# High parts of one expert weight and of four far-key tiles: from GpSimd to ScalarE

## The chip, the cores and the metric

One core of one Trainium2 chip. The metric is the device time of one execution in microseconds (us); several runs are taken and their median is shown. TensorE (PE), VectorE (DVE), ScalarE (ACT), GpSimd (POOL) and SyncE (SP, which issues the DMAs) each work through a queue of their own, in order.

## What is computed

Three stages, one after the other, on 2304 tokens of 512 features:

```python
scores = q @ k.T / sqrt(64)            # 4 batches, 8 heads, 576 positions, head size 64
scores = where(block_i >= block_j, scores, -1e9)   # causal by blocks of 64
x = softmax(scores) @ v                # -> x[2304, 512]
p = probs / probs.sum(-1)
y = sum_e p[:, e] * (relu(x @ w1[e]) @ w2[e])      # 4 experts, w1 512x1024, w2 1024x512
h = y @ w_in                           # 512 -> 1024
s = h * softmax(h)
out = layernorm(s) * g_ln @ w_out      # 1024 -> 512
```

## The kernel before, in words

Every operand of a matrix product is **split** into a high part (the value rounded to a narrower type) and a low part (what the rounding left), and a product takes three matmuls: high by high, high by low, low by high. So each weight, key, query, value and probability tile costs an instruction that makes the high part and one that makes the low part. Which engine makes which is written out by hand:

- **Weights**: `w_steps` (line 177) loads a weight into a staging tile of 128x4096, squares its four quarters on ScalarE to find a scale, and its inner `split` then makes, quarter by quarter (128x1024), the high part (GpSimd at L231 if `hi_eng is gp`, else ScalarE at L235) and the low part on VectorE (L238). On the ScalarE path `bg_` and `paced_a` may tie the instruction behind a marked ScalarE instruction in the schedule. The first expert's first weight is `next_w(gp)` at line 1241, its second one `next_w(gp, place_raw="w2")` at line 1242. All later weights already take ScalarE for the high part.
- **Keys and queries**: `parts` (line 788) makes high (L796 on ScalarE, L798 on GpSimd) and low (L800) by a two-letter `mode`: the first letter names the engine of the high part ("a" ScalarE, "p" GpSimd), the second that of the low part ("d" VectorE, "p" GpSimd). With `cut` it does so in two halves.
- **Far keys**: the first batch's keys come in two pieces. The near 192 columns are needed first (`k_near`), the far 384 (`k_far`, line 824, eight heads) from token tile 3 on. `k_far` uses mode "pp", so both parts are GpSimd's, 128x384 high and 64x384 low.

```python
if mode[0] == "a":
    act.activation(out=hi, in_=raw, func=AF.Copy)
else:
    gp.tensor_scalar(out=hi, in0=raw, scalar1=1.0, scalar2=1.0, op0=ALU.mult, op1=ALU.mult)
eng = vec if mode[1] == "d" else gp
eng.tensor_tensor(out=lo[ps], in0=raw[ps], in1=hi[ps], op=ALU.subtract)
```

**Order of the work.** `plan` (which the change touches) lists, for each step of attention, which loads and splits come with it; far keys of heads 0 and 1 come with step 6, 2 and 3 with step 7, and so on to step 9. A hand-written string of tokens sets the order of the first steps; after it a loop emits one attention step at a time, three background tasks (weight squares and splits) with each, and expert work between them by a running balance of costs. The order in which each engine finally gets its instructions is set by the scheduler of the framework, which runs a timing model of its own and follows dependencies and priorities; only SyncE's order is pinned in the first part. Raw key, raw value and similar loads share three buffers (`kr`), so a load waits in SyncE's queue until a GpSimd or ScalarE reader has released one.

One attention step is: scores on PE (`sps`, L920, L923), row maximum on VectorE (L935), its scaling (`nm`, L939), exponential on ScalarE (L979), probability split (`hl`: ScalarE L992, VectorE L993), a transposing DMA (`pT`), and the product with the values on PE (`pv`, L1021). The expert products are `hps` (L375) and `ops` (L397); the latter needs the second weight's four quarters.

Of the kernel before, what the change touches and what calls it, by code (L numbers as in the profile page):

```python
# [63 lines left out]
def tile_kernel(  # L64
# [38 lines left out]
    vec, act, gp, sync = nc.vector, nc.scalar, nc.gpsimd, InOrder(nc.sync)  # L103
# [8 lines left out]
    ap = ctx.enter_context(tc.tile_pool(name="acc", bufs=1))  # L112
# [609 lines left out]
    def next_w(hi_eng=None, eng=None, place_raw="stage"):  # L722
        i = nw[0]
        nw[0] += 1
        inv = iw[:, i:i + 1]
        tag, eng = f"w{i % 3}", eng or sync
        if i == 2 * len(LOADS):
            return w_steps("w_in", wf["w_in"], 15, inv, tag, eng)
        if i == 2 * len(LOADS) + 1:
            return w_steps("w_out", wf["w_out"], 15, inv, tag, eng, rows=gl)  # L730
        j, second = divmod(i, 2)
        j = LOADS[j]
        e = ORDER[j]
        key = ("w2" if second else "w1", e)
        if j >= E:
            inv = iw[:, 2 * e + second:2 * e + second + 1]
        pre, post = w_steps(
            key, (w2 if second else w1)[e], 15 if second else 10, inv, tag, eng, hi_eng=hi_eng, place_raw=place_raw,
            known=j >= E, less=j > E and not second,
        )  # L740
        return pre, [lambda: wcol.__setitem__(key, inv)] + post


    class Attention:
# [339 lines left out]
        def at(self, n, loads, *uses):  # L1084
            self.todo.append((n, loads, uses))

        def plan(self):
            first, at = self.first, self.at
            L = lambda f, *a: lambda: f(*a)
            for t in range(3, NTILE):  # L1090
                for c in range(2):
                    at(first[t] - 2 + 2 * c, ("qr", L(self.q_load, t, c)), L(self.q_prep, t, c))
            n = first[2]
            for h in range(NH):
                at(n + h // 2 + 2, ("kr", L(self.k_far_load, h)), L(self.k_far, h))
            for j in range(2, 5):
                at(first[j + 1] - 1, (None, None), L(self.v_split, 0, j))
            for b in range(1, NB):
                n = first[2 + 4 * b]
                f4 = n - 8  # L1100
                for j in range(5):
                    at(f4 - 5 + j, ("kr", L(self.v_load, b, j)), L(self.v_square, b, j))
                at(f4, (None, None), L(self.v_scale, b, 5))
                for j, m in enumerate([n - 2, n + LAG, n + LAG, n + LAG + 2, n + LAG + 3]):
                    at(m, ("kr", L(self.v_load, b, j)), L(self.v_split, b, j))
                for h in range(NH):
                    at(f4 + 1 + h, ("kr", L(self.k_load, b, h)), L(self.k_prep, b, h))
# [131 lines left out]
        xps[1].tile([128, 3, 512], F32, tag="xT1", name="vr"), xps[1].tile([128, 2, 512], F32, tag="xT3", name="vr"),  # L1239
    ]  # L1240
    p0, q0 = next_w(gp)
    p1, q1 = next_w(gp, place_raw="w2")

    def load_near(odd):
        at1.raws["near"] = near
        c = 0 if odd else S - NEAR
        src = kT[:, 0].rearrange("d (p x) s -> d p x s", x=2)[:, :, odd, c:c + NEAR]
        sync.dma_start(out=near.rearrange("d (p x) s -> d p x s", x=2)[:, :, odd], in_=src)

    def load_v(v, a, b):  # L1250
        sync.dma_start(out=v, in_=vC[0, :, a:b])
        for j in range(a, b):
            at1.raws["v", 0, j] = [v[:, j - a]]
# [5 lines left out]
    def norm():  # L1259
# [9 lines left out]
        n=[lambda: load_near(0), lambda: load_near(1)], v=[lambda: load_v(vrs[0], 0, 3), lambda: load_v(vrs[1], 3, 5)], p=[load_p],  # L1269
# [62 lines left out]
    p1, q1 = todo["x"], todo["X"]  # L1332
# [28 lines left out]
    for j in range(1, 5):  # L1361
        us = phase_units(j, GROUPS[j // E], psh)
        n = len(us)
# [46 lines left out]
    n = len(moe)  # L1410
# [209 lines left out]
```

## Time and profile before

| | |
|---|---|
| median of 3 runs | 1089.95 us (1089.48 to 1091.84) |
| the profiled execution | 1090.29 us |
| its span in the trace | 1088.5 us |
| PE busy | 1041.5 us, 96% of the span |
| VectorE busy | 776.3 us, 71% |
| ScalarE busy | 511.1 us, 47% |
| GpSimd busy | 208.1 us, 19%, 280 instructions |

How to read the rows below. In the page's picture of 40 slices a slice is 27.2 us and a digit the busy share in tenths. In the table by stretches the columns are: the stretch, its length, busy time (and instructions) of PE, PE's weight loads, VectorE, ScalarE and GpSimd, then the granted PE clock, the mean busy share of the DMA engines and GB/s. A line of a timeline is: start, duration, engine, source line, operation, tile written <- tiles read, and in brackets how long the engine had stood idle and what released it. A line of the chain is start, length and who held it. A line of a group of instructions is: source line, engine, operation, shapes, count, then busy time, mean ns of one, idle time before them.

### The profile page before, as it was taken

The numbers are of one execution on the slowest core, as the hardware profiler recorded it, in microseconds if no ns is written. First come the engines' busy times: TensorE is split into PE (matmuls) and PEld (weight loads), VectorE is DVE, ScalarE is ACT, GpSimd is POOL, SyncE is SP. The second block draws the span as 40 slices with busy tenths as digits, with TensorE's granted clock in tenths as the row PEclk, the third lists the DMA queues.
The fourth block names the chain that finished last, engine by engine and source line by source line (L and its number), as shares of the span: only waits on it lengthen the run. The fifth ranks groups of instructions, "written<-read, shape, count | busy, mean of one in ns | idle before, by whom it ended". The sixth has DMA issues, their size and how long they took to land.

```text
span 1088.5 us, 20680 instructions
## 1 busy us (share of the span) xinstructions
PE 1041.5 (96%) x8088; PEld 657.0 (60%) x8088; DVE 776.3 (71%) x1758; ACT 511.1 (47%) x1108; POOL 208.1 (19%) x280
## 2 busy tenths in 40 slices
PE   4679899999999999999899999999999999999998
PEld 4556666656655655655476777776766674444444
DVE  6879677748767765545786557665879558999883
ACT  5757578546755454532353334231446353323322
POOL 4967733534237311000000000000000000000000
PEclk9989999999999999999999999999999999999999
DMA  9978997566677865235331211330346312435233
GB/s 295 277 175 167 241 201 189 143 173 172 158 178 174 186 112 129 56 90 157 122 97 51 77 47 55 117 136 30 98 145 167 77 24 36 88 88 106 60 87 87
DMA packets 225745, 137.96 MB, mean 127 GB/s; under 512 B 184560, under 2 KB 193008, under 8 KB 225648
## 3 DMA queue, kind: packets, MB, share of 16 engines
q1 hardware_dynamic: 225648, 136.65, 50.3%
q8 instruction: 63, 1.03, 0.4%
q14 instruction: 34, 0.28, 0.1%
HBM read 79.47 MB, written 12.06 MB: 84 GB/s over the span
## 4 chain that ended last, share of the span: by engine, by line
PE 84%; DMA 6%; DVE 4%; POOL 3%; ACT 1%; issue 1%; SPq 0%; DVEq 0%; ACTq 0%; POOLq 0%
PE ops L397 31%; PE hps L629 14%; PE hps L375 14%; PE o L1536 9%; PE h L1470 9%; PE pv L1021 3%; DMA pT<-hl 3%; PE sps L920 2%; PE sps L923 2%; DMA xT<-xh 1%; POOL ks L800 1%; DMA raw<-in_w_dram 1%; DMA x2T<-xh 1%; DMA near<-in_kT_dram 1%; DMA vraw<-in_vC_dram 1%
## 5 line engine op out<-in xcount | busy, mean ns | idle before, releaser
L397 PE MATMUL ops<-wt,hch 128*128 128x512 f16 x1728 | 393.1, 379 | 2.4 <-DVE wt L238 1.4
L397 PEld LDWEIGHTS <-hch 128*128 128x128 f16 x1728 | 166.1, 98 | 187.4 <-issue 6.7
L375 PE MATMUL hps<-xT,wt 128*128 128x384 f16 (+1 forms) x1536 | 216.1, 290 | 6.3 <-DVE hch L386 3.9
L375 PEld LDWEIGHTS <-wt 128*128 128x128 f16 x1536 | 126.5, 100 | 64.4 <-issue 6.1
L979 ACT ACTIVATE p<-sps,nm 128x320 f32<-128x320 f32 (+3 forms) x120 | 70.1, 587 | 85.1 <-DVE nm L939 75.4
L993 DVE TENSOR_TENSOR hl<-p,hl 128x320 f16<-128x320 f32 (+3 forms) x120 | 75.6, 650 | 37.3 <-ACT hl L992 37.2
L629 PEld LDWEIGHTS <-S 128*128 128x128 f16 x1152 | 96.0, 98 | 3.0 <-issue 0.9
L1536 PE MATMUL o<-wt,lt 128*128 128x512 f16 (+1 forms) x456 | 95.6, 368 | 0.0
L1470 PE MATMUL h<-wt,x2T 128*128 128x512 f16 x432 | 95.5, 379 | 0.0
L238 DVE SCALAR_TENSOR_TENSOR wt<-stage,ws,wt 128x1024 f16<-128x1024 f32 (+1 forms) x64 | 82.9, 1304 | 7.4 <-ACT wt L235 4.3
L422 DVE SCALAR_TENSOR_TENSOR acc<-ops,coef,acc 128x512 f32<-128x512 f32 x54 | 40.4, 748 | 66.4 <-PE ops L397 66.3
L920 PE MATMUL sps<-ks,qhi 128*128 128x288 f32 (+3 forms) x160 | 69.1, 433 | 10.7 <-DVE hl L993 7.5
L629 PE MATMUL hps<-T,S 128*128 128x192 f16 x864 | 76.3, 246 | 0.0
L629 PEld LDWEIGHTS <-wt 128*128 128x128 f16 x864 | 72.8, 98 | 5.8
L642 ACT ACTIVATE stu<-hps 128x384 f32<-128x384 f32 x72 | 34.6, 482 | 86.5 <-PE hps L629 86.3
L1536 PEld LDWEIGHTS <-lt 128*128 128x128 f16 x456 | 44.6, 98 | 48.9
L1470 PEld LDWEIGHTS <-x2T 128*128 128x128 f16 x432 | 42.3, 98 | 51.0
L386 DVE SCALAR_TENSOR_TENSOR hch<-hps,hch 128x384 f16<-128x384 f32 (+1 forms) x98 | 52.8, 540 | 21.9 <-ACT hch L385 21.8
L647 ACT ACTIVATE hch<-stc 128x384 f16<-128x384 f32 x72 | 37.4, 521 | 63.5 <-DVE stc L655 63.2
L385 ACT ACTIVATE hch<-hps 128x384 f16<-128x384 f32 (+1 forms) x98 | 46.9, 481 | 39.5 <-PE hps L375 39.4
L1021 PE MATMUL pv<-v,pT 128*128 128x64 f16 x1392 | 56.6, 196 | 8.9 <-DMA pT<-hl 8.8
L1021 PEld LDWEIGHTS <-pT 128*128 128x128 f16 x1392 | 51.6, 100 | 20.5 <-DMA pT<-hl 10.8
(163 smaller groups left out, 1534.6 us busy)
## 6 DMA issues: line engine op xcount, KB each, us to landing
stage<-in_w_dram SPq DMA_DIRECT2D x50, 512.0 KB, 5.9
raw<-in_qT_dram SPq DMA_DIRECT2D x34, 256.0 KB, 3.1
vraw<-in_vC_dram SPq DMA_DIRECT2D x30, 256.0 KB, 3.2
raw<-in_kT_dram SPq DMA_DIRECT2D x24, 288.0 KB, 3.5
raw<-in_w_dram SPq DMA_DIRECT2D x24, 256.0 KB, 4.1
raw<-in_w_in_dram SPq DMA_DIRECT2D x8, 512.0 KB, 4.7
raw<-in_w_out_dram SPq DMA_DIRECT2D x8, 512.0 KB, 4.2
stage<-wf SPq DMA_DIRECT2D x8, 512.0 KB, 6.6
```

The lines of the kernel that those rows point to most:

```text
L238: stage["last"] = vec.scalar_tensor_tensor(out=lo, in0=r, scalar=stage[key, "s"], in1=hi, op0=ALU.mult, op1=ALU.subtract)
L375: pe.matmul(ps[:, j * n:j * n + n], w[:, a, kk, f * 128:(f + 1) * 128], x[:, b * KD + kk, c0:c0 + n], start=(m == 0), stop=(m == 3 * KD - 1),)
L385: marks["A"] = nc.scalar.activation(out=h[:, 0, :n], in_=ps[:, :n], func=AF.Relu)
L386: marks["D"] = nc.vector.scalar_tensor_tensor(out=h[:, 1, :n], in0=ps[:, :n], scalar=0.0, in1=h[:, 0, :n], op0=ALU.max, op1=ALU.subtract)
L397: pe.matmul(ps, hch[f][:, a, o0:o0 + 128], w[:, b, f, :], start=(m == 0), stop=(m == 3 * KF - 1))
L629: i = pe.matmul(ps[x][:, jj * HT:jj * HT + HT], lhs(a, kk, jj), rhs(b, kk), start=start, stop=(m == 5), skip_group_check=not first or jj > 0,)
L920: pe.matmul(o, q, rhs, start=True, stop=False)
L979: act.activation(out=src if direct else dst, in_=src, func=AF.Exp, bias=nm[:, j + x:j + x + 1], scale=SCALE, accum_out=sums[:, h:h + 1],)
L993: anc["D"] = vec.tensor_tensor(out=lo, in0=pf, in1=hi, op=ALU.subtract)
L1021: pe.matmul(o, tt[:, a * nch + c, :], v[:, bb, hs], start=(m == 0), stop=(m == total - 1))
L1470: pe.matmul(ps[:, half], x[:, a * KD + kk, c:c + 128], w[:, b, kk, half * 512:half * 512 + 512], start=(m == 0), stop=(m == 3 * KD - 1),)
L1536: pe.matmul(ps, tt[:, x * KF + f], w[:, y, f, c], start=(m == 0), stop=(m == 3 * KF - 1))
```

## The change

The far keys of the odd heads (four of eight) get mode "ap": ScalarE makes the high part, GpSimd still the low part. The first expert's second weight loses `gp`, so ScalarE makes its four high quarters. Nothing else is edited; the halves that `parts` cuts for later keys and queries are the same in both kernels.

```diff
             for h in range(NH):
-                at(n + h // 2 + 2, ("kr", L(self.k_far_load, h)), L(self.k_far, h))
+                at(n + h // 2 + 2, ("kr", L(self.k_far_load, h)), L(self.k_far, h, "ap" if h % 2 else "pp"))
...
     p0, q0 = next_w(gp)
-    p1, q1 = next_w(gp, place_raw="w2")
+    p1, q1 = next_w(place_raw="w2")
```

## Rows read from the trace of the kernel before

**Rows 1.** The page's picture of the span in 40 slices.

```profile
PE   4679899999999999999899999999999999999998
...
POOL 4967733534237311000000000000000000000000
```

**Rows 2.** The table by stretches.

```profile
50.00:57.00 7.00, 5.14 (x76) 4.56 (x74) 6.85 (x18) 5.18 (x14) 6.92 (x7) 1.00 0.59 185
57.00:66.40 9.40, 7.21 (x61) 4.09 (x59) 6.62 (x12) 2.80 (x10) 9.11 (x9) 1.00 0.50 120
66.40:76.40 10.00, 7.21 (x78) 6.14 (x76) 7.50 (x17) 7.46 (x22) 7.09 (x9) 0.73 1.03 211
...
82.00:136.00 54.00, 47.95 (x645) 36.76 (x644) 43.28 (x92) 35.43 (x87) 41.69 (x58) 1.00 0.94 202
136.00:1088.50 952.50, 942.46 (x6984) 576.77 (x6981) 670.15 (x1516) 422.98 (x869) 109.70 (x158) 1.00 0.45 112
```

**Rows 3.** The chain that ended last: first and last of 25 pieces on GpSimd, and the next.

```profile
33.72 2.08 POOL wt L231
...
60.54 2.10 POOL ks L800
62.66 2.78 DMA vraw<-in_vC_dram
```

**Rows 4.** Groups of GpSimd's instructions, 50 to 72 us.

```profile
L231 POOL TENSOR_SCALAR wt<-stage,ws 128x1024 f16<-128x1024 f32 x4 | 4.9, 1221 | 0.2
...
L798 POOL TENSOR_SCALAR ks<-raw 128x384 fp32r<-128x384 f32 x5 | 3.7, 745 | 0.0
```

**Rows 5.** GpSimd's timeline, two low parts of far keys.

```profile
60.54 2.09 POOL L800 TENSOR_TENSOR ks<-raw,ks 64x384 fp32r<-64x384 f32 x1
...
70.01 0.99 POOL L800 TENSOR_TENSOR ks<-raw,ks 64x384 fp32r<-64x384 f32 x1
```

**Rows 6.** VectorE's timeline around the second weight's low parts.

```profile
50.20 0.15 DVE L143 RECIPROCAL ws<-iw 128x1 f32<-128x1 f32 x1
...
60.49 1.28 DVE L238 SCALAR_TENSOR_TENSOR wt<-stage,ws,wt 128x1024 f16<-128x1024 f32 x1 [1.48 <-POOL wt L231]
61.70 0.15 DVE L939 TENSOR_SCALAR nm<-sps 128x2 f32<-128x2 f32 x1
...
63.89 1.52 DVE L238 SCALAR_TENSOR_TENSOR wt<-stage,ws,wt 128x1024 f16<-128x1024 f32 x1 [1.30 <-POOL wt L231]
```

**Rows 7.** PE's timeline, its waits for the second weight and the far keys.

```profile
61.83 1.24 PE L397 MATMUL ops<-wt,hch 128*128 128x512 f16 x5 [0.94 <-DVE wt L238]
...
68.11 0.41 PE L920 MATMUL sps<-ks,qhi 128*128 128x320 f32 x1 [0.46 <-POOL ks L800]
...
71.05 0.64 PE L920 MATMUL sps<-ks,qhi 128*128 128x320 f32 x1 [1.61 <-POOL ks L800]
```

**Rows 8.** The table by stretches, finer, where the granted clock falls.

```profile
68.00:72.00 4.00, 1.97 (x17) 1.34 (x17) 3.58 (x10) 3.45 (x10) 3.06 (x5) 0.88 1.15 150
72.00:76.00 4.00, 3.59 (x41) 3.45 (x42) 2.38 (x5) 2.13 (x7) 2.51 (x4) 0.50 1.11 323
76.00:80.00 4.00, 4.00 (x55) 3.35 (x54) 2.47 (x8) 2.75 (x10) 0.00 (x0) 0.77 1.11 215
```

**Rows 9.** ScalarE: group and single instructions that price the added work.

```profile
L235 ACT ACTIVATE wt<-stage,ws 128x1024 f16<-128x1024 f32 x4 | 4.6, 1148 | 0.0
...
L992 ACT ACTIVATE hl<-p 128x320 f16<-128x320 f32 x8 | 3.4, 460 | 0.0
```

**Rows 10.** ScalarE's timeline, two single instructions.

```profile
5.13 0.63 ACT L796 ACTIVATE qhi<-qv 128x512 fp32r<-128x512 f32 x1 [3.12 <-DMA qv<-in_qT_dram]
...
61.88 0.53 ACT L979 ACTIVATE p<-sps,nm 128x320 f32<-128x320 f32 x1 [4.78 <-DVE nm L939]
```

**Rows 11.** SyncE's last load of a far key, and such loads' time to landing.

```profile
60.04 0.53 SPq L94 DMA_DIRECT2D raw<-in_kT_dram  x1
...
raw<-in_kT_dram SPq DMA_DIRECT2D x8, 192.0 KB, 3.4
```

## The prediction

> **What bounds the kernel now.** I read the picture of the span first. PE is busy in nine tenths of nearly every slice, but not in the first three, and there GpSimd reaches its peak, nine tenths in the second slice [rows 1]. So PE sets the pace of the rest, and time can be won only where PE stands idle early on. The table by stretches says how much: from 57.0 to 66.4 us PE is idle for 9.40 - 7.21 = 2.19 us, from 66.4 to 76.4 for 10.00 - 7.21 = 2.79, together 4.98. From 82 to 136 it is idle for 6.05 us, and in all the 952.5 us that follow for 10.0 [rows 2].
>
> Next the chain that ended last. From 33.72 to 62.64 us it stays on GpSimd for 25 pieces, and goes on by a raw-value load [rows 3]. GpSimd's queue is thus the bound of that stretch: in 50 to 66.4 it is busy for 6.92 + 9.11 of 16.4 us, while ScalarE works 5.18 + 2.80 [rows 2]. The timelines show how the queue reaches PE. VectorE stands 1.48 and 1.30 us for a high quarter of the second weight, and the scaling of a row maximum (L939) is queued behind such a low quarter; ScalarE's exponential waits for that scaling with 4.78 us of idleness before it [rows 6, 10]. PE itself waits 0.94 us for the weight and 0.46 and 1.61 us for far keys [rows 7].
>
> The price of these waits does not end with the waits: the granted clock falls to 0.50 of full speed, the lower of the two levels (1.2 GHz), in 72 to 76, after PE was busy only 1.97 us of the 4 before [rows 8].
>
> **The change part by part.** The sum is made against the profiled execution's own 1090.29 us; the median of the runs is 0.34 lower, so the last step takes 0.34 off.
>
> *Removed from GpSimd.* Four high quarters of the weight, 4.9 us by their group. Four far-key high parts, by the mean of the five in the same stretch 4 x 0.745 = 3.0 us [rows 4]. Its queue gets 7.9 us shorter before the last far key, whose low part now begins at 70.01 and ends at 71.0 [rows 5].
>
> *Added to ScalarE.* Four quarters at 1.148 us, the price of the same instruction for later weights: 4.6 us. Four high parts of 128x384: no row has this size with this output; below stands 0.460 for 320 columns, above 0.63 for 512 columns of the same output type. I take 0.52, nearer to the first in size, so 2.1 us; ends 1.8 and 2.5 [rows 9, 10]. The 6.7 us lie beside other work: ScalarE has 7.00 - 5.18 + 9.40 - 2.80 = 8.4 us free from 50 to 66.4 [rows 2], 4.78 of them in one piece before the exponential [rows 10]. If that cover is gone, the exponentials pay (third rival).
>
> *The first term: VectorE no longer waits for GpSimd.* The scale `ws` is there at 50.35 [rows 6]. Even if all of ScalarE's 5.18 us of 50 to 57 go first [rows 2], the third quarter is ready by 50.35 + 5.18 + 3 x 1.148 = 59.0 and the fourth by 60.1; VectorE now begins the third low quarter at 60.49 and the fourth at 63.89. The two waits of 1.48 and 1.30 go, and the second scaling behind them, its exponential, its transpose and the `pv` that waits for this move up by 2.78 us. Nothing on VectorE is added: it makes the same low parts. What is late next is VectorE itself, busy 6.85 of 7.00 us in 50 to 57 [rows 2]. So -2.8; ends 0 (the exponentials lose on ScalarE what VectorE wins) and -2.8.
>
> One row speaks of a further gain: a far-key low part on GpSimd took 2.09 us where the last took 0.99, and it began 0.05 us after VectorE began a low quarter of 1.28 [rows 5, 6]. So these two delay each other, and fewer instructions on GpSimd may mean shorter ones on VectorE. I count nothing for it in the sum; one quarter took 1.52 and another 1.28 [rows 6], so if all four of VectorE's low quarters lost that difference it would be 4 x 0.24 = 1.0 us, which I keep for the lower end. The Trainium skill, "SBUF — State Buffer", section "SBUF: two separate sides", holds that GpSimd and VectorE instructions with two SBUF inputs exclude each other for a whole instruction, while ScalarE never waits; the trace agrees in that one pair (2.09 against 0.99), and by the rule the first term would be nearer to -3.8 than to -2.8.
>
> *The second term: far keys.* PE's waits of 0.46 and 1.61 us [rows 7] go, since GpSimd's queue ends 7.9 us earlier, or as early as the last load allows: it is issued at 60.04, once a GpSimd low part has released the buffer, and lands 3.4 us later [rows 11]. SyncE's queue moves up with the buffers, as does the raw-value load behind them at 62.66 [rows 3]. But the `pv` and scores behind these waits hang on the exponentials as well, and those move up only by the first term. So I count 0 beyond it; ends 0 and -2.2 (4.98 us of idleness less 2.8).
>
> *The third term: the clock.* At the full level the 3.59 us in 72 to 76 would be 1.8 shorter, the 4.00 in 76 to 80 by 0.23 x 4.0 = 0.9, and the 1.97 before by 0.12 x 1.97 = 0.2 [rows 8]. That is 2.9 us, if PE no longer stands idle for 2.03 of 4 us ahead of them. The first term takes away more than half of the 4.98 us of idleness, so I take half: -1.5; ends 0 and -2.9.
>
> *The edits' other ends.* The first odd far key's high part leaves GpSimd before 43 us too, ahead of the value splits; a part's time, 0.745 us, is the most that it can win, and I count it at nothing, for the bound only. No DMA is added or removed.
>
> Sum: -2.8 - 1.5 = -4.3, so 1086.0 on the profiled execution's scale and **1085.7** on the median's. At the far end -2.8 - 1.0 - 2.2 - 2.9 - 0.7 = -9.6.
>
> **The rivals.** What a measurement of this kernel can tell from no change is about 0.2%, 2.2 us.
>
> *The transposes give it back.* DMA is busy for 1.03 of its time from 66.4 to 76.4 and 0.94 from 82 to 136 [rows 2]. If those transfers end when they do now, PE comes earlier and waits there: the idle 6.05 us of 82 to 136 would grow by what was won. Against this: the DMA engines are at 0.59 and 0.50 in 50 to 66.4 [rows 2], because their issues wait for GpSimd's buffers; they can start earlier too. By this rival some 1 us is left: 1089.0.
>
> *ScalarE in GpSimd's place.* ScalarE's queue is in order. If the four weight quarters (4.6), two far keys (1.0) and a wait for the last far-key load (it lands at 60.04 + 3.4 = 63.4, 1.5 us after the exponential at 61.88) stand in one block ahead of that exponential, this is 7.1 us against 4.78 of idleness [rows 9 to 11]. It decides from the point where the exponential starts later than 61.88, and costs 7.1 - 4.78 = 2.3 us, passed to PE through `pv`: 1092.3, slower. Against it: the far keys of the later heads are emitted steps later, and a scheduler by readiness would put the exponential ahead of a far key that has not landed.
>
> *The change doesn't do what it says* is nearly excluded: without `gp`, `split` has the ScalarE path that every later weight uses, and four such instructions are in the trace [rows 9]. The scheduler may however order other things anew; that can win or lose part of the 10.0 us of idleness behind 136 us [rows 2], and is why the chances aren't higher.
>
> **How the numbers follow.** My forecast, GpSimd's chain shortened and most of it kept: 0.60. The transposes, or something like them, give it back to within 0.2%: 0.22. ScalarE in GpSimd's place, or a worse order: 0.18. The time is that of the likeliest, 1085.7. The range goes from 1081.5, which leaves out only the case that nearly every far end comes true (1080.4), up to 1092.3, the third rival's time; the forecast's own range is 1081.5 to 1087.8. Faster by over 0.2% 0.60, within 0.2% 0.22, slower by over 0.2% 0.18.
>
> **What would show it.** After the change GpSimd should have eight instructions fewer and some 8 us less work, and the chain should leave it before 55 us. VectorE's waits for GpSimd at L238 should be gone; PE's idleness in 57 to 76 should fall from 4.98 to about 2, and the stretch at half clock be shorter. The products with the second weight should end some 3 us earlier. I am wrong if the exponential at 61.88 starts no earlier, if ScalarE shows a weight quarter or a far key with idleness ahead of it just before an exponential, or if PE's waits for `pT` behind 82 us grow by what the front wins.

## The result, and the profile after

The changed kernel is **slower** by 0.8%: 1099.27 us median (1094.09 to 1103.96, 5 runs) against 1090.06 (1089.48 to 1091.98, 5 runs), ratio of the means 1.0077 with 95% interval [1.0047, 1.0106]. The forecast was 1085.7 with a range up to 1092.3. The profiled execution took 1100.92 us, its span is 1099.1 us, 10.6 more than before.

The page of the changed kernel, busy times:

```profile
PE 1046.4 (95%) x8088; PEld 660.6 (60%) x8088; DVE 775.0 (71%) x1758; ACT 516.7 (47%) x1116; POOL 196.9 (18%) x272
```

GpSimd lost its 8 instructions and 208.1 - 196.9 = 11.2 us. PE has the same 8088 matmuls as before and is busy 1046.4 - 1041.5 = 4.9 us longer, at a lower clock (0.989 granted on the mean over the span, 0.997 before). The other 10.6 - 4.9 = 5.7 us are idleness. The table by stretches says where (stretch, length, busy time of PE, PE's weight loads, VectorE, ScalarE, GpSimd, granted clock, DMA share, GB/s):

```profile
50.00:57.00 7.00, 3.71 (x44) 3.16 (x41) 6.43 (x12) 7.00 (x15) 5.53 (x6) 0.79 0.64 189
57.00:66.40 9.40, 9.40 (x75) 5.44 (x74) 6.39 (x13) 7.35 (x20) 4.22 (x7) 0.80 0.78 199
66.40:76.40 10.00, 10.00 (x131) 7.50 (x128) 7.64 (x22) 8.72 (x26) 2.81 (x5) 1.00 0.72 180
76.40:82.00 5.60, 3.63 (x36) 2.21 (x33) 4.99 (x14) 4.12 (x6) 0.00 (x0) 1.00 1.21 159
82.00:136.00 54.00, 46.43 (x595) 38.00 (x596) 37.58 (x80) 31.73 (x79) 34.80 (x52) 0.91 0.89 188
136.00:200.00 64.00, 56.51 (x597) 39.55 (x595) 45.02 (x100) 45.77 (x116) 27.18 (x37) 0.95 0.87 191
200.00:1099.10 899.10, 890.68 (x6417) 540.51 (x6414) 627.64 (x1421) 378.89 (x762) 88.54 (x126) 1.00 0.42 106
```

and the stretch of the kernel before that [rows 2] holds only as part of a longer one:

```profile
136.00:200.00 64.00, 61.99 (x634) 41.04 (x631) 46.64 (x105) 47.93 (x117) 21.42 (x33) 1.00 0.83 195
```

From 57.0 to 76.4 us PE's idleness fell from 4.98 us [rows 2] to 0: more than was forecast. But it grew on either side: from 7.00 - 5.14 = 1.86 to 3.29 us in 50 to 57, and from 0 to 1.97 in 76.4 to 82. Two waits make this (PE's timeline, changed kernel):

```profile
55.14 0.61 PE L920 MATMUL sps<-ks,qhi 128*128 128x320 f32 x1 [3.29 <-DVE hl L993]
...
82.92 0.70 PE L1021 MATMUL pv<-v,pT 128*128 128x64 f16 x18 [2.89 <-DMA pT<-hl]
```

The front as a whole, first before, then after the change:

```profile
50.00:82.00 32.00, 25.16 (x282) 19.41 (x279) 24.62 (x54) 19.91 (x58) 23.11 (x23) 0.89 0.77 188
```

```profile
50.00:82.00 32.00, 26.73 (x274) 18.32 (x270) 25.45 (x58) 27.18 (x66) 12.55 (x16) 0.89 0.80 184
```

By 82 us PE has gained 26.73 - 25.16 = 1.57 us at the same mean clock, 0.89, where the forecast was 4.3. From 136 to 200 its idleness rose from 64.00 - 61.99 = 2.01 to 64.00 - 56.51 = 7.49, from 82 to 136 from 6.05 to 7.57, together by 7.0 us, and the clock there was no longer 1.00. Behind 200 us idleness is as it was (8.4 us against 888.5 - 880.47 = 8.0 in the kernel before). So the front won a part of what was foretold, and the stretch from 82 to 200 us, where no moved instruction stands, cost several times as much.

The front first. The timelines of the changed kernel, ScalarE's exponential and then VectorE:

```profile
59.05 0.56 ACT L979 ACTIVATE p<-sps,nm 128x320 f32<-128x320 f32 x1
...
51.55 1.77 DVE L238 SCALAR_TENSOR_TENSOR wt<-stage,ws,wt 128x1024 f16<-128x1024 f32 x1 [0.54 <-ACT wt L235]
...
58.06 0.14 DVE L939 TENSOR_SCALAR nm<-sps 128x2 f32<-128x2 f32 x1
...
58.30 1.26 DVE L238 SCALAR_TENSOR_TENSOR wt<-stage,ws,wt 128x1024 f16<-128x1024 f32 x1
```

The exponential begins 61.88 - 59.05 = 2.83 us earlier than before [rows 10]. VectorE no longer waits for GpSimd at L238 [rows 6]; but note that the scaling of the row maximum (L939) now stands ahead of the third low quarter, where it stood behind it. The order of VectorE's queue is another. GpSimd's last piece in the front of the chain that ended last is at 43.25 us instead of 60.54 [rows 3]; from there the chain runs over VectorE and, at 50.48 us, over the first moved quarter on ScalarE (L235, 1.05 us).

Now the back. PE's waits by what ended them, first of the changed kernel (us in total, times, longest), then of the one before:

```profile
PE pv L1021 <- DMA pT<-hl: 16.9, 9, 3.8
```

```profile
PE pv L1021 <- DMA pT<-hl: 8.8, 6, 2.3
```

The same behind 82 us alone, changed kernel first (it counts the wait of 2.89 us that ends at 82.92):

```profile
PE pv L1021 <- DMA pT<-hl: 14.6, 8, 3.8
```

```profile
PE pv L1021 <- DMA pT<-hl: 5.9, 4, 2.3
```

PE's timeline around the largest of them, changed kernel:

```profile
147.68 0.51 PE L1021 MATMUL pv<-v,pT 128*128 128x64 f16 x12
148.03 1.03 PE L397 MATMUL ops<-wt,hch 128*128 128x512 f16 x4
149.87 0.42 PE L920 MATMUL sps<-ks,qhi 128*128 128x320 f32 x1 [0.81 <-ACT p L979]
...
150.69 0.20 PE L925 MATMUL sps<-mc,mr 128*128 128x64 bf16 x1
154.66 1.14 PE L1021 MATMUL pv<-v,pT 128*128 128x64 f16 x18 [3.77 <-DMA pT<-hl]
156.89 3.71 PE L375 MATMUL hps<-xT,wt 128*128 128x128 f16 x39 [1.09 <-DMA xT<-xh]
```

and the same place in the kernel before:

```profile
142.52 0.51 PE L1021 MATMUL pv<-v,pT 128*128 128x64 f16 x12
142.87 4.70 PE L397 MATMUL ops<-wt,hch 128*128 128x512 f16 x21
147.22 0.50 PE L920 MATMUL sps<-ks,qhi 128*128 128x320 f32 x1
...
148.12 0.20 PE L925 MATMUL sps<-mc,mr 128*128 128x64 bf16 x1
150.19 2.18 PE L375 MATMUL hps<-xT,wt 128*128 128x128 f16 x36 [1.87 <-DMA xT<-xh]
152.21 0.69 PE L1021 MATMUL pv<-v,pT 128*128 128x64 f16 x18
```

Before, 21 expert products (4.70 us) stand between two pairs of scores and 36 more between the scores and the `pv`; the exponential, split and transpose are done while PE works on them. (This `pv` needs the pair of scores ahead of the first gap: the other pair's exponentials begin only at 150.86 us, and at 153.12 after the change.) After the change 4 products are left in the first gap and none in the second: the 39 stand behind the `pv`. PE waits 3.77 us, and its clock falls to 0.57, near the lower of the two levels (1.2 GHz), in the stretch around the end of this wait:

```profile
152.00:160.00 8.00, 4.25 (x50) 4.14 (x50) 3.70 (x12) 4.29 (x13) 1.53 (x2) 0.57 0.82 207
```

Where the missing products went, two source lines tell: ScalarE takes the first expert's outputs of the first tokens (L417) at 68.72, 84.94, 99.66 and 121.50 us, before the change at 69.60, 90.16, 110.55 and 129.54. Expert work was pulled ahead by up to 10.9 us, while attention's finished tiles (L1063) came at 87.00, 110.58 and 139.56 us instead of 89.19, 107.59 and 135.71: a lead of 2.2 us became a lag of 3 to 4. The order in which PE gets its matmuls differs between the two programs from about 52 us to about 200 us, though the edit touches no matmul.

### The profile page after: what moved, and what is told of

Its sections match the earlier page's. It is cut to its first block, busy times and chain, and to the rows that moved or that the text cites. A ratio compares the mean times of both kernels' runs of the same rounds, so it can differ in the third digit from the quotient of the medians.

```text
span 1099.1 us, 20684 instructions
## 1 busy us (share of the span) xinstructions
PE 1046.4 (95%) x8088; PEld 660.6 (60%) x8088; DVE 775.0 (71%) x1758; ACT 516.7 (47%) x1116; POOL 196.9 (18%) x272
## 4 chain that ended last, share of the span: by engine, by line
PE 79%; DMA 8%; DVE 6%; ACT 2%; issue 2%; POOL 1%; SPq 1%; DVEq 0%; ACTq 0%; POOLq 0%
PE ops L397 30%; PE hps L629 14%; PE hps L375 11%; PE o L1536 8%; PE h L1470 8%; DMA pT<-hl 5%; PE pv L1021 3%; PE sps L920 2%; PE sps L923 1%; DVE hl L993 1%; DVE hch L386 1%; DMA xT<-xh 1%; DVE v L882 1%; DMA x2T<-xh 1%; DVE sps L935 1%
## 5 line engine op out<-in xcount | busy, mean ns | idle before, releaser
L238 DVE SCALAR_TENSOR_TENSOR wt<-stage,ws,wt 128x1024 f16<-128x1024 f32 (+1 forms) x64 | 82.9, 1304 | 7.1 <-ACT wt L235 6.8
L920 PE MATMUL sps<-ks,qhi 128*128 128x288 f32 (+3 forms) x160 | 69.3, 434 | 11.2 <-DVE hl L993 9.4
```

The source lines that it names most:

```text
L238: stage["last"] = vec.scalar_tensor_tensor(out=lo, in0=r, scalar=stage[key, "s"], in1=hi, op0=ALU.mult, op1=ALU.subtract)
L920: pe.matmul(o, q, rhs, start=True, stop=False)
```

## The experiments

All but two hold an order fixed. At the end of the emission a call was added that ties each listed instruction of an engine to the one listed before it, with dependencies that carry no wait on the chip; engines not listed are left to the scheduler, and so are the eight moved instructions where nothing else is said.

```diff
             m2_o(t - OLAG)
+    pin_order(tc)
```

Of each run the table gives the ratio to the kernel before, and PE's idleness (length less busy time) and granted clock from the table by stretches.

| run | ratio [95%] | idle 82-136 | idle 136-200 | clock 136-200 |
|---|---|---|---|---|
| before | 1 | 6.05 | 2.01 | 1.00 |
| after | 1.0077 [1.0047, 1.0106] | 7.57 | 7.49 | 0.95 |
| engines_new_order_old | 0.9998 [0.9983, 1.0013] | 6.25 | 2.15 | 1.00 |
| engines_old_order_new | 1.0120 [1.0096, 1.0143] | 8.67 | 6.78 | 0.93 |
| weight_alone | 1.0082 [1.0064, 1.0100] | 5.68 | 7.36 | 0.92 |
| keys_alone | 1.0038 [1.0027, 1.0050] | 4.92 | 4.74 | 0.97 |
| loads_late | 1.0129 [1.0108, 1.0151] | 9.29 | 7.79 | 0.93 |
| sp_order_old | 1.0104 [1.0084, 1.0124] | 9.65 | 6.34 | 0.95 |
| pe_order_old | 1.0036 [1.0022, 1.0051] | 7.21 | 2.19 | 1.00 |
| old_engines_pe_order_new | 1.0110 [1.0088, 1.0131] | 8.80 | 6.85 | 0.94 |
| pe_order_new_to_100us | 1.0035 [1.0020, 1.0049] | 9.39 | 1.98 | 0.97 |
| pe_order_new_to_134us | 1.0057 [1.0037, 1.0077] | 8.03 | 6.12 | 0.92 |
| pe_order_new_from_134us | 1.0100 [1.0082, 1.0118] | 7.16 | 5.88 | 0.95 |
| order_old_loads_first | 1.0005 [0.9990, 1.0020] | 5.69 | 2.13 | 1.00 |
| order_old_scalar_by_hand | 1.0013 [0.9999, 1.0028] | 6.10 | 2.01 | 1.00 |
| order_old_both_by_hand | 0.9979 [0.9964, 0.9994] | 5.49 | 2.13 | 1.00 |
| order_old_vector_by_hand | 0.9994 [0.9980, 1.0008] | 5.69 | 2.09 | 1.00 |
| engines_old_vector_by_hand | 1.0009 [0.9995, 1.0023] | 6.14 | 2.42 | 1.00 |

### Is it the engines or the order?

**engines_new_order_old**: the changed kernel with every queue in the order of the kernel before. **engines_old_order_new**: the kernel before with every queue in the order of the changed one.

> The changed kernel, with every engine's instructions held in the order that they had in the kernel before; only the eight moved high parts find their own place in ScalarE's queue. Theory 'order' (the move itself helps, the loss comes from the new order that the scheduler made of everything else): 1083 to 1088 us, with no wait of VectorE for GpSimd at L238 and the weight loads behind the transposes as before. Theory 'engine' (ScalarE in GpSimd's place costs the time): 1094 us or more, with weight quarters or far keys on ScalarE ahead of exponentials.

> The kernel before, with every engine's instructions held in the order of the changed kernel; the eight high parts stay on GpSimd. Theory 'order': slower than before, 1097 to 1110 us, as it has the new order and not what the move wins. Theory 'engine': near the time before, 1088 to 1092 us.

The second came as theory 'order' had it (1104.68 us, ratio 1.0120); the first, 1091.06 us and 0.9998, lies between the two theories. The new order loses without any work moved, and with the old order the moved work neither loses nor wins. Whether the move wins anything in the new order is not shown. 1.0077 against 1.0120 would be 0.4% or 4.7 us, but it sets a run without a held order against one with it, and loads_late below, the changed kernel with its own order held but for four loads, took 1.0129. Why the move wins nothing in the old order, these lines of engines_new_order_old show (GpSimd, VectorE, ScalarE):

```profile
63.23 0.51 POOL L798 TENSOR_SCALAR ks<-raw 128x384 fp32r<-128x384 f32 x1 [6.64 <-DMA raw<-in_kT_dram]
...
60.84 1.27 DVE L238 SCALAR_TENSOR_TENSOR wt<-stage,ws,wt 128x1024 f16<-128x1024 f32 x1
62.04 0.15 DVE L939 TENSOR_SCALAR nm<-sps 128x2 f32<-128x2 f32 x1
...
59.80 0.38 ACT L385 ACTIVATE hch<-hps 128x256 f16<-128x256 f32 x1 [0.61 <-PE hps L375]
60.08 1.14 ACT L235 ACTIVATE wt<-stage,ws 128x1024 f16<-128x1024 f32 x1
64.37 0.52 ACT L796 ACTIVATE ks<-raw 128x384 fp32r<-128x384 f32 x1 [3.15 <-DMA raw<-in_kT_dram]
64.80 0.51 ACT L979 ACTIVATE p<-sps,nm 128x320 f32<-128x320 f32 x1
```

VectorE's waits for GpSimd are gone and the third high quarter is ready at 58.16, but the third low quarter still begins at 60.84, after 60.49 before [rows 6]: it stands behind the low parts of the relu pieces (`hch`), and ScalarE makes the third of these at 59.80, where it did so at 56.72 before. That ScalarE's queue order does this, the run order_old_scalar_by_hand below supports: with two far keys, a quarter and the two background squares put behind relu pieces, the third low quarter begins at 58.88. (The squares stood ahead of them before the change too, so the run does not price the moved work alone.) Then ScalarE, in order, stands 3.15 us for the last far key's load right ahead of the exponential, which begins at 64.80 instead of 61.88: the mechanism of the third rival.

### Which half of the edit?

**weight_alone** and **keys_alone** make one of the two edits, with nothing held.

```diff
-    p1, q1 = next_w(gp, place_raw="w2")
+    p1, q1 = next_w(place_raw="w2")
```

```diff
-                at(n + h // 2 + 2, ("kr", L(self.k_far_load, h)), L(self.k_far, h))
+                at(n + h // 2 + 2, ("kr", L(self.k_far_load, h)), L(self.k_far, h, "ap" if h % 2 else "pp"))
```

> Only the second weight's high parts on ScalarE, order left to the scheduler. Theory 'order': the sign hangs on the order that comes out, not on the work moved; if the next weight's loads are again issued before the transposes of the fourth and fifth tiles, 1094 to 1103 us, if not 1085 to 1091. Theory 'engine': two thirds of the added ScalarE work, so about 1096 us.

> Only the odd far keys' high parts on ScalarE, order left to the scheduler. Theory 'order': again by the order that comes out, anywhere in 1085 to 1100 us. Theory 'engine': a third of the added ScalarE work, so about 1093 us.

Either loses by itself, 0.82% and 0.38%, and both show idleness in 136 to 200 (7.36 and 4.74 us). Theory 'engine' had about 1096 and 1093 us; measured were 1100.36 and 1095.57. The two losses sum to 1.2%, and both edits together cost 0.77%, so they don't read as a price per instruction moved. That each edit brings an order of its own fits this, but these two orders were not held or compared.

### Which queue's order?

**loads_late** keeps all orders of the changed kernel, but puts four loads of the next weight, which SyncE had issued ahead of the transposes at 89 us, behind the next four `pT` transposes. **pe_order_old** and **sp_order_old**: the changed kernel with only PE's, or only SyncE's, order of before. **old_engines_pe_order_new**: the kernel before with only PE's order of the changed one.

> The changed kernel in its own order on every engine, but for four DMAs: the four 512 KB loads of the next expert weight stand in SyncE's queue behind the transposes of the tile with 448 keys, where the kernel before had them, and not ahead of them. Theory 'loads ahead of transposes': the lead of about 6 us that the changed kernel has over the one before at 86 us is kept past 102 us, and the time falls by 4 to 6 us against the changed kernel, to 1093 to 1096. Theory 'PE order' (expert products were done early, and nothing is left to fill the waits for transposes later): 1097 to 1101, the lead is lost further on all the same.

> The changed kernel with only PE's instructions held in the order of the kernel before; the scheduler orders the other engines around that. Theory 'PE order': the loss is gone and the far-key loads, free to go early, let the move win what the front lost: 1082 to 1088 us. Theory 'other engines' order': still 1094 us or more.

> The changed kernel with only SyncE's queue of DMAs held in the order of the kernel before. Theory 'loads ahead of transposes' (SyncE's order is the cause): 1088 to 1092 us, less whatever the move wins. Theory 'PE order': 1094 us or more, as PE's order is again the scheduler's own.

> The kernel before (high parts on GpSimd) with only PE's instructions held in the order of the changed kernel. Theory 'PE order': as slow as with all orders new, 1100 to 1106 us. Theory 'other engines' order': 1088 to 1094 us.

Loads ahead of transposes are not it (1.0129, no better), nor is SyncE's order (1.0104). PE's order carries the larger part of the loss: its new order alone, on the old engines, costs 1.1%, and its old order takes the idleness of 136 to 200 back from 7.49 to 2.19 and the ratio to 1.0036. That is 1093.91 us, which neither theory had (1082 to 1088, or 1094 and more): nearly half of the 0.77% stays. Waits in front go with it: `pv` waits 3.78 us for a transposed tile at 73.29 us and 1.73 at 85.71, the first of which before was 0.72. SyncE's and ScalarE's queues had been ordered anew there.

### Which stretch of PE's order?

PE's list was put together from the two orders: the new one up to a point and the old one from there, or the other way round.

> The changed engines; PE follows the order of the changed kernel for its first 659 matmuls' worth of work (to about 100 us of its trace), and from there the order of the kernel before, skipping what is done; all other engines are left to the scheduler. Expert products are thus up to 9.8 us ahead of the attention at about 91 us, as in the changed kernel, and level with the order of before again from about 120 us. Theory F (the loss is the price of the filler used up early): most of the loss stays, ratio 1.006 to 1.010, with PE's waits for transposes in 100 to 136 us. Theory L (the loss lies in the order behind 120 us, where the changed kernel presses attention together until the expert products are 12 us behind): ratio no worse than the 1.0036 of the run with all of PE's order of before, 0.999 to 1.004, and PE's idleness in 136 to 200 near the 2.0 us of before.

> The changed engines; PE follows the order of the kernel before up to the attention product that begins at 134.29 us in its trace, and from there the order of the changed kernel; all other engines are left to the scheduler. Up to the cut this is the run with all of PE's old order (1.0036). Theory L (some half of the loss lies in the new order behind 100 us, where attention is pressed together): the loss of the changed kernel shows although nothing was pulled ahead in front, PE idles 5 to 8 us in 136 to 200 instead of 2.0, ratio 1.006 to 1.010. Theory M (the later order costs only because of the state in which the front leaves the queues): PE's idleness in 136 to 200 stays near 2, ratio 1.002 to 1.005.

> The changed engines; PE follows the order of the changed kernel up to the attention product that begins at 138.23 us in its trace (the one at 134.29 us in the trace of before), and from there the order of the kernel before; all other engines are left to the scheduler. This is the complement of pe_order_new_from_134us (1.010). Theory L (what the changed kernel loses is lost behind that point, where only 4 expert products stand between two pairs of scores instead of 21 and the product with the values follows right behind the scores): the 3.77 us wait at 154 us and the fall of the clock there don't come, PE idles about 2 us in 136 to 200, ratio 0.999 to 1.003. Theory F (what was pulled ahead in front is missing later wherever it is): waits of 3 us or more come at some other place behind 134 us, ratio 1.005 to 1.009.

With the new order up to 100 us the ratio is 1.0035, the same as with none of it: pulling expert products ahead in front does not cost the second half of the loss, if the old order follows early enough. With the new order only from 134 us on it is 1.010, and its PE timeline repeats the place shown above, scores and then at once the `pv`:

```profile
149.72 0.20 PE L925 MATMUL sps<-mc,mr 128*128 128x64 bf16 x1
153.55 1.14 PE L1021 MATMUL pv<-v,pT 128*128 128x64 f16 x18 [3.62 <-DMA pT<-hl]
154.50 4.10 PE L375 MATMUL hps<-xT,wt 128*128 128x128 f16 x39
```

So that stretch of the order costs by itself. But the complement, which has the old order from 134 us on, is not free: 1.0057, with new places to stand, also behind that point (PE's timeline):

```profile
129.09 1.05 PE L1021 MATMUL pv<-v,pT 128*128 128x64 f16 x30 [3.83 <-DMA pT<-hl]
142.34 0.21 PE L1021 MATMUL pv<-v,pT 128*128 128x64 f16 x1 [3.33 <-POOL v L881]
156.55 3.32 PE L375 MATMUL hps<-xT,wt 128*128 128x128 f16 x36 [2.70 <-DMA xT<-xh]
```

Here theory F came true in its numbers (1.0057, and 3.33 us at 142.34), though that wait is for a value tile of GpSimd (L881); theory L did not: the named wait went, and others of its size came. With the new order up to 100 us it was the other way round: L came true, F (1.006 to 1.010) did not. So neither explains all three runs, and the parts of the loss don't add (0.57 and 1.0 against 0.77%). What all runs share is the column 136 to 200: 2.0 to 2.4 us of idleness in each run whose ratio is 1.0036 or less, 5.9 to 7.8 in each of 1.0057 or more, and keys_alone between the two with 1.0038 and 4.74 us. Which rule of the scheduler made that order was not tried, and why the waits come at just these places with mixed orders stays open.

### Is the forecast gain there in the old order?

Five runs keep PE's and GpSimd's old order, so that only the other queues in the front differ; four of them have the changed engines. **order_old_loads_first** moves two far-key loads on SyncE ahead of three transposes:

```diff
+L94 DMA raw<-in_kT_dram 128x384 x2
 L94 DMA_TRANSPOSE xT<-xh 128x8x128
 L94 DMA_TRANSPOSE pT<-hl 128x6x128
-L94 DMA raw<-in_kT_dram 128x384
 L94 DMA_TRANSPOSE pT<-hl 128x6x128
-L94 DMA raw<-in_kT_dram 128x384
```

**order_old_scalar_by_hand** orders ScalarE's queue instead, against engines_new_order_old (both orders as the traces have them), and on VectorE moves one reduction (L217), which needs the two background squares (L132 `junk`), behind the second L939:

```diff
 L979 ACTIVATE sps<-sps,nm 128x192
-L796 ACTIVATE ks<-raw 128x384
 L979 ACTIVATE sps<-sps,nm 128x192
 L1074 ACTIVATE xh<-xf,xs 128x512
 L992 ACTIVATE hl<-sps 128x192
-L796 ACTIVATE ks<-raw 128x384
 L992 ACTIVATE hl<-sps 128x192
 L385 ACTIVATE hch<-hps 128x384
-L235 ACTIVATE wt<-stage,ws 128x1024
-L132 ACTIVATE junk<-stage 128x1024
+L796 ACTIVATE ks<-raw 128x384
 L385 ACTIVATE hch<-hps 128x384
-L235 ACTIVATE wt<-stage,ws 128x1024
-L132 ACTIVATE junk<-stage 128x1024
+L796 ACTIVATE ks<-raw 128x384
+L235 ACTIVATE wt<-stage,ws 128x1024 x2
 L385 ACTIVATE hch<-hps 128x256
 L235 ACTIVATE wt<-stage,ws 128x1024
-L796 ACTIVATE ks<-raw 128x384
 L979 ACTIVATE p<-sps,nm 128x320 x2
 L992 ACTIVATE hl<-p 128x320 x2
+L132 ACTIVATE junk<-stage 128x1024 x2
+L796 ACTIVATE ks<-raw 128x384
```

**order_old_both_by_hand** does both. **order_old_vector_by_hand** adds the swaps below on VectorE, and on ScalarE puts the second pair of exponentials ahead of the two squares. **engines_old_vector_by_hand** does the VectorE swaps alone, on the unchanged engines:

```diff
-L1075 SCALAR_TENSOR_TENSOR xh<-xf,xs,xh 128x512
 L993 TENSOR_TENSOR hl<-sps,hl 128x192 x2
+L1075 SCALAR_TENSOR_TENSOR xh<-xf,xs,xh 128x512
...
+L939 TENSOR_SCALAR nm<-sps 128x2
 L238 SCALAR_TENSOR_TENSOR wt<-stage,ws,wt 128x1024
-L939 TENSOR_SCALAR nm<-sps 128x2
```

> The changed engines with all orders of the kernel before, except that SyncE's two last far-key loads stand ahead of the three transposing DMAs instead of between them. In the run with every order of before, ScalarE stood 3.15 us for the last of these loads right ahead of the exponential, which began at 64.80 us instead of 61.88. Theory A (the first term was there, and this wait ate it): the wait goes, the exponential starts at about 62.2 (the scaling of the row maximum ends at 62.2 in that run), and the ratio to the kernel before falls from 0.9998 to about 0.9975 to 0.9990. Theory B (what the front wins is given back at the transposes from 82 us on): the exponential is earlier as in A, PE's idleness in 57 to 76 falls, that in 82 to 136 grows by as much, and the ratio stays within 0.999 to 1.001.

> The changed engines with the orders of the kernel before on PE, GpSimd and SyncE; on ScalarE the moved quarters and far keys stand behind the relu pieces (L385) instead of ahead of them, and the last far key and two background squares stand behind the two exponentials; on VectorE the reduction of those squares (L217) stands behind the second scaling of the row maximum. In the run with every order of before the relu pieces began 1.5, 2.4 and 3.1 us later than before, and VectorE's third low quarter, queued behind the same pieces, began at 60.84, no earlier than the 60.49 of before. Theory A (the first term is real once ScalarE's queue doesn't eat it): the third low quarter begins at about 59, the exponential at about 60.5 instead of 61.88, ratio 0.996 to 0.9985. Theory B (the transposes give it back): the exponential is earlier as in A, but the ratio is within 0.999 to 1.001, with PE's idleness of 82 to 136 grown by what 57 to 76 lost.

> Both edits together: the two far-key loads ahead of the three transposing DMAs, and ScalarE's queue by hand as in the run before this one. Theory A: the exponential at about 60.5 and the last far keys' products no longer late, so the whole of the forecast sum can show: ratio 0.995 to 0.998. Theory B: within 0.999 to 1.001.

> As order_old_both_by_hand (0.9979), and on VectorE the two scalings of the row maximum (L939) stand ahead of the third and fourth low quarters instead of behind them, two probability low parts (L993) ahead of the low part of x (L1075); on ScalarE the second pair of exponentials ahead of the two background squares. Theory A (the exponentials' start is still what counts): the first at about 58.7 instead of 59.83, the second pair at about 62.5 instead of 65.04, PE's wait of 2.77 us for a transposed tile at 71 us falls to under 1, ratio 0.995 to 0.997. Theory B (transposes and PE's own work bound the stretch by now): the exponentials move as in A, but the wait for transposed tiles is only shifted to a later place, ratio 0.997 to 0.999.

> The engines of the kernel before and every order of it, but for VectorE's three swaps of the run before this one (row maximum's scaling ahead of the low quarter, twice; probability low parts ahead of the low part of x). Theory A (the first term is the wait of the scaling behind a low quarter that waits for GpSimd): the exponential moves from 61.88 to about 59.2 without any work moved to ScalarE, PE still waits for the weight's quarters, ratio 0.997 to 0.9995. Theory C (the weight quarters and far keys on GpSimd are themselves the bound): PE's waits at the second weight and the far keys stay, ratio 0.999 to 1.001.

Each moves the exponential about as expected: to 62.01, 60.25, 59.83, 58.95 and 59.89 us, against 64.80 with the old order and 61.88 before. The time follows only partly: 1.0005, 1.0013, 0.9979, 0.9994, 1.0009. Only the third ratio lies in the range of its theory A; the first is in that of B and the last in that of C, and the other two are in none. With both edits, PE's idleness in 57 to 76.4 is 2.77 us (about 2 were forecast; in 50 to 57 it is 2.60, up from 1.86), and that in 82 to 136 does not grow (5.49):

```profile
50.00:57.00 7.00, 4.40 (x48) 3.77 (x46) 5.42 (x15) 6.59 (x15) 4.17 (x5) 0.78 0.49 173
57.00:66.40 9.40, 9.40 (x65) 5.34 (x64) 7.99 (x12) 7.58 (x19) 6.47 (x8) 0.80 0.70 147
66.40:76.40 10.00, 7.23 (x97) 6.33 (x96) 6.46 (x17) 7.97 (x24) 2.54 (x5) 0.83 1.00 221
...
82.00:136.00 54.00, 48.51 (x666) 38.01 (x663) 44.02 (x93) 35.44 (x88) 41.18 (x56) 1.00 0.94 205
```

So the first rival (transposes give it back) is not what happens there. This is the one version whose interval lies below 1, by 0.06 to 0.36%, and it beats the changed kernel by far more. The next edit did not add to it: the second pair of exponentials came at 63.68 (62.5 was expected), PE's wait of 2.77 us fell to 2.21 (under 1 was expected), and the ratio's interval holds 1 again. Its profiled span is the shortest of all, 1084.8 us, but its 12 runs have the median 1088.51 against 1089.99 of the kernel before. One interval of five that just misses 1 makes a gain likely and doesn't show it. That the work must leave GpSimd for it is not settled either: VectorE's order alone, on the old engines, brought the first exponential to 59.89 and no time (1.0009); PE then still waits 0.94, 0.84 and 0.41 us for the weight and 0.46 and 1.61 for far keys, as before [rows 7].

## Why the prediction was wrong

- **The bound and the chain: right, but what lay next was missed.** GpSimd held the front; it left the chain there (last piece at 43.25 us), and PE's idleness of 57 to 76.4 went from 4.98 to 0. But 1.43 and 1.97 us of idleness came on either side, for a probability low part and a transposed tile, so that 1.57 us were won by 82 us. The first tokens' products with the second weight, which should have ended some 3 us earlier, ended at 67.66 us instead of 66.70.
- **First term, -2.8: right for the exponential in the changed kernel** (2.83 us earlier), **but by another way than the one worked out, and not as time won.** With the old order the same edit made it 2.92 us later (64.80 against 61.88). The part got the start of the third low quarter from the weight alone (59.0 for the quarter, which was ready at 58.16); the low quarter began at 60.84, because VectorE's queue puts a relu piece ahead of it, and the relu pieces were pushed back in ScalarE's queue by the very work that was to cost nothing. With two far keys, a quarter and the squares put behind them by hand it began at 58.88. That this is near 59.0 is luck: the high quarter was ready at 57.04, and a relu piece, at 58.54, set the start again. "The 6.7 us lie beside other work" was checked against free time, not against who is queued behind: that step failed, and only the scheduler's new order hid it.
- **Second term, 0: right for the sum.** The far keys' waits at PE are gone in the changed kernel.
- **Third term, -1.5: not there.** The low clock of 72 to 76 us [rows 8] is gone, 66.4 to 76.4 is at 1.00, but 50 to 57 is at 0.79 and 57 to 66.4 at 0.80, where it was 1.00: it came earlier, after PE had been idle for 7.00 - 3.71 = 3.29 us. Over 50 to 82 us the mean is 0.89 as before. Behind 82 us, where the clock had been 1.00, it fell three more times: to 0.86 in 96 to 104, and to 0.57 in 128 to 136 and in 152 to 160.
- **The step that failed and decided: "The scheduler may however order other things anew; that can win or lose part of the 10.0 us of idleness behind 136 us."** It got no term in the sum, only a share in the chance of 0.18. The bound was wrong in kind: existing idleness bounds what a new order can win, not what it can add. Behind 136 us idleness rose from 10.0 to 963.1 - 947.19 = 15.9 us, from 82 to 136 by 1.5, and PE's matmuls took 4.9 us longer at the lower clock. engines_old_order_new prices the step: +1.2%, some 13 us, with no work moved.
- **The rivals.** ScalarE in GpSimd's place is what the edit does when the order is held, though the time there was level with before, not 2.3 us above it. The transposes: the sign that was named, PE's waits for `pT` behind 82 us, came and was larger than the gain in front (14.6 us instead of 5.9). The way that was put, PE early and the transfers as before, is not the one at the largest wait: the scores that this `pv` needs came some 5 us later than before (their last matmul at 147.64 us against 142.49), and most of the products that had stood behind them were gone. The slower end of the range, 1092.3, left out the cause that decided; the faster end, 1081.5, is not added up from any terms.

## What to carry to other kernels

Where a scheduler orders the queues, an edit of two lines is two edits: the work moved, and a new order of everything behind it. Price the second by holding the order of before and changing the engines, and the reverse, and hold each kernel's own order once too, so that held runs are set against held runs; if the two differ by more than the gain in view, the engine assignment is not what is being measured. Free time on the engine that takes the work is not a cover: list what is queued behind the moved instruction and which engine waits for that, and look for an instruction that waits for a load just ahead of a critical one.

## What the runs showed that was not expected

The same kernel's executions spread more than the effect looked for: order_old_both_by_hand ran from 1083.66 to 1090.21 us in 12 runs, with granted clocks of 0.994 to 1.000 over the span.

VectorE's low quarter takes 1.27 us alone and up to 2.10 beside GpSimd's key low parts (engines_new_order_old). In order_old_both_by_hand GpSimd's began 0.02 us ahead of VectorE's (their timelines):

```profile
61.94 2.07 DVE L238 SCALAR_TENSOR_TENSOR wt<-stage,ws,wt 128x1024 f16<-128x1024 f32 x1
...
61.92 1.00 POOL L800 TENSOR_TENSOR ks<-raw,ks 64x384 fp32r<-64x384 f32 x1
```

The quarter is 0.80 us longer than alone, while GpSimd's piece keeps its 1.00. That agrees with the rule named in the prediction (the Trainium skill, "SBUF — State Buffer", section "SBUF: two separate sides"). In the pair that the prediction read [rows 5, 6] only GpSimd's piece, which began second, was late; VectorE's kept 1.28, so "these two delay each other" said too much. The use of the rule there, that fewer GpSimd pieces would shorten VectorE's, did not come: moved ahead to 51 to 58 us, the remaining key low parts met the first two low quarters, which took 1.77 and 1.75 us in the changed kernel; all four took 6.06 us instead of 5.83.

The clock fell after idleness even where PE was then busy throughout: in order_old_both_by_hand it stood at 0.62 in 57 to 62 us with 5.00 of 5.00 us busy, after 2.60 us of idleness in the 7 us before.
